# Softcap attention and two mixers on one core: the second block of keys added onto the first by a transfer, the softmax sums in three passes

## The chip, the core and the metric

The kernel runs on one core of one Trainium2 chip. The core has five engines, each with its own queue of instructions, which it works through in order: TensorE (PE, matrix products), VectorE (DVE), ScalarE (ACT), GpSimd (POOL) and SyncE (SP), which here issues transfers. Sixteen DMA engines move data between HBM and SBUF, the on-chip memory. The metric is the device time of one execution in microseconds; less is better.

## The reference

Three layers follow each other. This is the first, the one that the change touches, for 4 batches, 12 heads, 448 positions and 64 channels per head:

```python
scores = scale * np.matmul(q, k.transpose(0, 1, 3, 2))
scores = cap * np.tanh(scores / cap)
scores = scores - np.max(scores, axis=-1, keepdims=True)
attn = np.exp(scores)
attn = attn / (np.sum(attn, axis=-1, keepdims=True) + 1e-09)
return np.matmul(attn, v).astype(np.float32)
```

The second layer mixes tokens and then channels by two pairs of matrices each with a ReLU between; the third takes the real part of a two-dimensional Fourier transform, normalises, and applies two more matrices, 768 to 3072 and back. All is float32.

## The kernel before

Attention works on 12 quads, four heads each: a quad is one batch and a third of its heads, held as two pairs. The 448 keys stand on the partitions, in three blocks of 128 (`KC = 3`) and a rest of 64, and the 448 queries run along the free dimension. The first three blocks of a pair lie in one tile `t` of shape [128, 3, 2, 448] (block, head of the pair, query); the rests of both pairs share one tile `te`. There are four buffers for `t`, so two quads can be under way.

For each pair, TensorE makes the scores of one block of both heads (line 630, tile `sc`), ScalarE takes the tanh out of PSUM into `t` (line 616). VectorE takes the maximum over the blocks (through line 435, tile `m`), GpSimd takes it over the partitions, one all-reduce per head (line 670, tile `mb`), VectorE subtracts (line 435) and ScalarE takes the exponential in place (line 678). Then TensorE makes two products from the exponentials:

- the values (`av`, line 731, one product per pair, 12 matmuls of 32 columns of weights; line 741 adds the rest keys of both pairs);
- the softmax sums (`den`, line 766, one product per quad). Its weights `marks` hold ones in chosen columns, so that each of the four heads' sums over the keys lands in 32 partitions of its own. It runs over the three blocks and the rest: four passes of four matmuls.

ScalarE copies both out of PSUM (tile `xt`), TensorE turns the results (line 785), VectorE divides by the sums (line 823). As batches are finished, the token mixer of the second layer runs between the quads (lines 404 to 406 in `mix1` with tile `mx`, lines 886 and 890 in `mix2`). The channel mixers and the transform follow; they hold three quarters of the time, almost all of it matrix products of lines 404 to 406 with tile `mm`.

The order of all work is written down. Each piece is recorded with `pl.op`, with what it reads and writes; a table `ORDER` of 4192 numbers gives the sequence in which the pieces are issued, and a set `POOLED` names the pieces that GpSimd does where two engines could. The costs in `pl.op` (`{"T": 3.0}`, `lag=2.1`) do nothing when the program is built; the table was drawn up with them. Within an engine the instructions run in the order of the table, each waiting for what it reads and for its buffers to come free.

Of the kernel before, what the change touches and what calls it, by code (L numbers as in the profile page):

```python
# [16 lines left out]
ALU = mybir.AluOpType  # L17
# [7 lines left out]
KC = 3  # L25
# [33 lines left out]
class Op:  # L59
# [305 lines left out]
def kernel(  # L365
# [17 lines left out]
    V, A, P, T = nc.vector, nc.scalar, nc.gpsimd, nc.tensor  # L383
# [159 lines left out]
    def phase_ab(heads, mixer, banks_a, banks_b):  # L543
# [210 lines left out]
        def normed(stage, b, q, eks, te, sums):  # L754
            ps = ps_new(av_p, "av", [128, 512])
            twin = q < 2
            at = (32, 0, 16)[q]
            stage("den")

            def den(e):  # L760
# [1410 lines left out]
```

## Time and profile before

| | |
|---|---|
| time, median of 3 runs (lowest, highest) | 1335.45 us (1333.64, 1335.49) |
| profiled execution, its own time | 1332.71 us |
| its span, first to last instruction | 1330.6 us |
| mean granted TensorE clock | 0.999 of 2.4 GHz |
| PE busy | 1311.3 us, 99% |
| DVE busy | 992.6 us, 75% |
| ACT busy | 773.4 us, 58% |
| POOL busy | 479.5 us, 36% |
| DMA | 239.20 MB, mean 180 GB/s |

How to read it: the profile is of one execution, so its times are compared with its own 1332.71 us, 2.1 us over the span, and not with the median. Busy time of an engine leaves out register, semaphore and DMA-issuing instructions. Matmuls are pipelined and their ends are modelled, so the mean duration of one record is longer than the time by which it moves the next one back; where several follow each other, the pieces of the chain of waits, which lie end to end, give the time that they take together. A float32 matmul has two records, so `x24` of the value product are 12 matmuls. Matmuls on the rounded format (lines 404 to 406 and 890) and the turns have one.

### The profile page before, as it was taken

To read this page: it belongs to the slowest core of one execution; us is meant where nothing else is said; L and a number is where in the kernel's file an instruction comes from. 1 tells how busy PE (TensorE), PEld (TensorE's weight loads), DVE (VectorE), ACT (ScalarE), POOL (GpSimd) and SP (SyncE) were. 2 spreads that over 40 slices of the span, in tenths; PEclk is the share of its full clock that TensorE was granted. 3 is DMA by queue.
4 is the path that set the end of the run, shared out by engine and by line. 5 is a ranking of instruction groups with operands and counts; after the bars stand their busy time and mean duration, and the time that the engine had idled before them with its cause. 6 is when DMAs were issued, how large, how long until landed. Compare 5 with 4: busy or idle time off the path is not lost.

```text
span 1330.6 us, 18417 instructions
## 1 busy us (share of the span) xinstructions
PE 1311.3 (99%) x7214; PEld 1094.2 (82%) x7214; DVE 992.6 (75%) x1038; ACT 773.4 (58%) x934; POOL 479.5 (36%) x244
## 2 busy tenths in 40 slices
PE   7999999999999999999999999999999999999998
PEld 3345454589999999999999999999999999999997
DVE  7998888746655666577998866757889738558798
ACT  8898887778667666454545424553554454544432
POOL 4443426112322011323323554634533544412322
PEclk9999999999999999999999999999999999999999
DMA  4222211056888888997766753455565743323332
GB/s 164 104 88 96 68 57 42 1 196 223 314 293 299 268 304 276 325 308 261 293 215 233 252 183 109 141 177 184 185 217 174 268 146 100 122 100 109 105 108 83
DMA packets 74328, 239.20 MB, mean 180 GB/s; under 512 B 8354, under 2 KB 10274, under 8 KB 74114
## 3 DMA queue, kind: packets, MB, share of 16 engines
q1 hardware_dynamic: 74240, 238.03, 51.7%
q8 instruction: 57, 0.93, 0.3%
q14 instruction: 29, 0.24, 0.0%
q10 hardware_dynamic: 2, 0.00, 0.0%
HBM read 171.77 MB, written 69.56 MB: 181 GB/s over the span
## 4 chain that ended last, share of the span: by engine, by line
PE 84%; DVE 7%; ACT 5%; POOL 2%; DMA 2%; issue 1%; SPq 0%; POOLq 0%; DVEq 0%; ACTq 0%
PE mm L404 24%; PE mm L405 24%; PE mm L406 24%; PE sc L630 2%; PE av L731 2%; DVE t L435 2%; DVE m L435 2%; PE mx L890 2%; POOL mb L670 1%; ACT t L616 1%; ACT t L678 1%; PE av L766 1%; PE av L785 1%; DMA kept<-p 1%; PE mx L886 1%
## 5 line engine op out<-in xcount | busy, mean ns | idle before, releaser
L435 DVE TENSOR_TENSOR z<-mm,z 128x896 f32<-128x896 f32 (+1 forms) x207 | 198.8, 976 | 86.9 <-PE mm L406 83.2
L405 PE MATMUL mm<-u,wh 128*128 128x448 f32 x564 | 206.1, 365 | 0.0
L404 PE MATMUL mm<-u,wh 128*128 128x448 f32 x552 | 201.9, 366 | 0.0
L406 PE MATMUL mm<-u,wl 128*128 128x448 f32 x552 | 201.7, 365 | 0.0
L406 PE MATMUL mm<-r,wl 128*128 128x448 f32 x498 | 182.1, 366 | 1.1 <-DMA wl<-kept 1.1
L404 PE MATMUL mm<-r,wh 128*128 128x448 f32 x498 | 182.3, 366 | 0.7 <-DVE z L435 0.4
L435 POOL TENSOR_TENSOR p<-p 128x768 f32<-128x768 f32 (+1 forms) x47 | 91.9, 1955 | 246.6 <-DMA kept<-p 87.5
L405 PE MATMUL mm<-r,wh 128*128 128x448 f32 x462 | 169.0, 366 | 0.0
L670 POOL PARTITION_ALL_REDUCE mb<-m x48 | 105.2, 2239 | 148.4 <-DVE m L435 118.2
L432 ACT ACTIVATE r<-mm 128x896 fp32r<-128x896 f32 (+5 forms) x87 | 71.3, 829 | 144.4 <-PE mm L406 124.8
L405 PEld LDWEIGHTS mm<-u,wh 128*128 128x128 f32 x564 | 106.0, 188 | 8.7
L404 PEld LDWEIGHTS mm<-u,wh 128*128 128x128 f32 x552 | 103.6, 188 | 8.7
L406 PEld LDWEIGHTS mm<-u,wl 128*128 128x128 f32 x552 | 103.7, 188 | 8.5
L406 PEld LDWEIGHTS mm<-r,wl 128*128 128x128 f32 x498 | 93.5, 188 | 9.3 <-DMA wl<-kept 1.5
L404 PEld LDWEIGHTS mm<-r,wh 128*128 128x128 f32 x498 | 93.5, 188 | 9.0 <-DVE z L435 0.8
L432 ACT ACTIVATE cv<-raw 128x768 bf16<-128x768 int8 (+2 forms) x76 | 67.6, 889 | 52.0 <-DMA raw<-in_m_dram 39.6
L405 PEld LDWEIGHTS mm<-r,wh 128*128 128x128 f32 x462 | 86.8, 188 | 7.8 <-DVE r L966 0.7
L435 DVE TENSOR_TENSOR t<-t,mb 128x1344 f32<-128x1344 f32 x48 | 82.0, 1721 | 10.5 <-POOL mb L670 10.2
L405 PE MATMUL mm<-u,raw 128*128 128x448 f32 x246 | 89.8, 365 | 0.0
L435 POOL TENSOR_TENSOR wl<-wl,wh 128x768 fp32r<-128x768 f32 x29 | 58.7, 2030 | 72.6 <-ACT wh L432 72.6
L404 PE MATMUL mm<-u,raw 128*128 128x448 f32 x216 | 79.0, 366 | 0.3 <-DVE z L435 0.3
L406 PE MATMUL mm<-u,raw 128*128 128x448 f32 x216 | 78.9, 365 | 0.0
(245 smaller groups left out, 3011.8 us busy)
## 6 DMA issues: line engine op xcount, KB each, us to landing
raw<-in_m_dram SPq DMA_DIRECT2D x48, 768.0 KB, 6.3
kept<-p SPq DMA_DIRECT2D x96, 384.0 KB, 5.0
wl<-kept SPq DMA_DIRECT2D x82, 384.0 KB, 3.6
raw<-kept SPq DMA_DIRECT2D x53, 384.0 KB, 3.1
raw<-in_c_dram SPq DMA_DIRECT2D x24, 768.0 KB, 6.2
p<-kept SPq DMA_DIRECT2D x35, 384.0 KB, 4.0
qr<-in_qk_dram SPq DMA_DIRECT2D x23, 448.0 KB, 4.7
wh<-kept SPq DMA_DIRECT2D x24, 384.0 KB, 5.1
```

Of the source, the lines that this page charges most:

```text
L404: T.matmul(out=dst, lhsT=wh, rhs=xh, start=first, stop=False, skip_group_check=more)
L405: T.matmul(out=dst, lhsT=wh, rhs=xl, start=False, stop=False, skip_group_check=more)
L406: T.matmul(out=dst, lhsT=wl, rhs=xh, start=False, stop=last, skip_group_check=more)
L432: pl.op(a(n), lambda e: A.activation(out=out(), in_=src(), func=func, **kw), reads, writes)
L435: pl.op(engs, lambda e: eng[e].tensor_tensor(out=out(), in0=in0(), in1=in1(), op=op), reads, writes)
L616: pl.op(a(W2, 0.06), lambda e: A.activation(out=out(), in_=ps()[:, :, :S], func=AF.Tanh, scale=scl[:, 0:1]), [ps, "cap", *reads], writes)
L630: T.matmul(out=ps()[:, k, :S], lhsT=qr()[d, S + c * 128:S + (c + 1) * 128], rhs=qr()[d, :S], start=True, stop=True)
L670: pl.op({"P": 1.9}, lambda e, k=k: P.partition_all_reduce(mb()[:, k], mx()[:, k], 128, bass_isa.ReduceOp.max), [mx, mb], [kb], hold=0.75)
L678: pl.op(a(KC * S, 0.1), lambda e, k=k: A.activation(out=tl()[:, :, k], in_=tl()[:, :, k], func=AF.Exp, scale=cap_sb[:, 0:1]), [tl, "cap"], ...
L731: T.matmul(out=ps()[d, :S], lhsT=vv()[:, KC * p + c, d], rhs=tl()[:, c, hd], start=(c == 0), stop=False, skip_group_check=True)
L766: T.matmul(out=ps()[32 * k:32 * k + 32, :S], lhsT=w, rhs=tl()[:, c, hd] if c < KC else te()[:, hd], start=(c == 0), stop=(c == KC))
L890: T.matmul(out=ps()[:, :S], lhsT=channels_of(rt()[:, tb, c], kc % NJ), rhs=wt[:, tb, :], start=False, stop=last, skip_group_check=True)
```

## The change

After the value products of a quad, two transfers are issued from GpSimd's queue, one per pair. Each adds `t[:, 1]`, the exponentials of the second block of keys, onto `t[:, 0]`, those of the first, in SBUF (`accum_op=ALU.add`, 128 partitions of 896 numbers, 448 KB). The sums product then runs over block 0, block 2 and the rest: three passes, 12 matmuls. The value product needs the first block unsummed, so the transfer waits for it (through the key `(t, "sum")`, which the value product reads and the transfer writes) and for the two exponentials; the sums product waits for both transfers.

```diff
 POOLED = {
-    23, 26, 32, 35, 82, 85, 91, 94, 139, 142, 148, 151, 214, 217, 223, 226, 281, 284, 290, 293, 338, 341, 347, 350,
...
+    23, 26, 32, 35, 46, 47, 84, 87, 93, 96, 107, 108, 143, 146, 152, 155, 166, 167, 220, 223, 229, 232, 243, 244, 289,
...
-                pl.op({"T": 2.25}, av, [vv] + [x for tl, hd, ke in ts for x in (tl, ke)], [ps], mode="cols")
+                pl.op({"T": 2.25}, av, [vv] + [x for tl, hd, ke in ts for x in (tl, ke)] + [(ts[0][0], "sum")], [ps], mode="cols")
...
             at = (32, 0, 16)[q]
+            stage("pre")
+            sums_in = []
+            for ts in eks:
+                (tl, _, k0), (_, _, k1) = ts
+                pl.op({"P": 0.7}, lambda e, tl=tl: P.dma_start(out=tl()[:, 0], in_=tl()[:, 1], accum_op=ALU.add),
+                      [tl, k0, k1], [(tl, "sum")], lag=4.0)
+                sums_in.append((tl, "sum"))
             stage("den")
 
             def den(e):
-                for c in range(KC + 1):
+                for c in (0, 2, KC):
...
-            pl.op({"T": 3.0}, den, [te, (te, "e")] + [x for ts in eks for tl, hd, ke in ts for x in (tl, ke)], [ps], mode="cols")
+            pl.op({"T": 2.3}, den, [te, (te, "e")] + sums_in + [x for ts in eks for tl, hd, ke in ts for x in (tl, ke)], [ps], mode="cols")
```

`ORDER` has 4216 numbers now, 24 more for the transfers, and was drawn up anew, so the sequence differs over the whole kernel. Lines of the changed kernel have numbers higher by 2 up to the transfer (line 764 there) and by 9 after it. Three places matter most.

The first is TensorE around the sums product of the first quad: `av` the values, `te` the rest keys, `marks` the sums, `sc` scores of later quads. Before:

```order
L731 MATMUL av<-t,v 32x448 x12
L630 MATMUL sc<-qr 128x448 x4
L731 MATMUL av<-t,v 32x448 x12
L741 MATMUL av<-te,v 64x448 x4
L766 MATMUL av<-t,marks 32x448 x12
L766 MATMUL av<-te,marks 32x448 x4
L630 MATMUL sc<-qr 128x448 x2
```

The same place of the changed kernel:

```order
L733 MATMUL av<-t,v 32x448 x12
L632 MATMUL sc<-qr 128x448 x2
L733 MATMUL av<-t,v 32x448 x12
L743 MATMUL av<-te,v 64x448 x4
L632 MATMUL sc<-qr 128x448 x6
L775 MATMUL av<-t,marks 32x448 x8
L775 MATMUL av<-te,marks 32x448 x4
L632 MATMUL sc<-qr 128x448 x2
```

Three score steps (6 matmuls) have moved in between the second value product and the sums product.

The second place is TensorE in the fourth quad, where the token mixer's products (`mx`) run between. Before:

```order
L731 MATMUL av<-t,v 32x448 x12
L741 MATMUL av<-te,v 64x448 x4
L630 MATMUL sc<-qr 128x448 x2
L766 MATMUL av<-t,marks 32x448 x12
L766 MATMUL av<-te,marks 32x448 x4
```

The same place of the changed kernel:

```order
L733 MATMUL av<-t,v 32x448 x12
L632 MATMUL sc<-qr 128x448 x2
L895 MATMUL mx<-ident,x 128x112 x4
L899 MATMUL mx<-w2h,rh 128x448
L899 MATMUL mx<-w2h,rl 128x448
L899 MATMUL mx<-w2l,rh 128x448
L899 MATMUL mx<-w2h,rh 128x448
L899 MATMUL mx<-w2h,rl 128x448
L899 MATMUL mx<-w2l,rh 128x448
L743 MATMUL av<-te,v 64x448 x4
L632 MATMUL sc<-qr 128x448 x2
L775 MATMUL av<-t,marks 32x448 x8
```

A score step and a whole output block of the mixer stand there in addition. In the other quads the filling is of the same kind: score steps (two matmuls each), turns (four matmuls of line 794 there), mixer products. From the end of the second value product to the sums product stand, in quads 3 to 12: 12 mixer products of the first kind, `te` and 2 score steps; 1 score step, 1 output block, `te`, 1 step; 1 step, 1 block, `te`, 2 steps; `te`, 2 steps, 12 first-kind products, 4 turns; 1 step, 1 block, `te`, the rest's step; 12 first-kind products, 1 step, `te`, 1 step; 1 block, `te`, 2 steps, 4 turns; 1 step, 12 first-kind products, `te`, 1 step; 1 step, `te`, 1 block, 12 first-kind products; `te` and 2 blocks.

The third place is GpSimd's queue from the first to the fourth quad; `mb` is an all-reduce, its number that of the pair. Before:

```order
L670 ISA mb_339<-m2_323 128x448 x2
L670 ISA mb_378<-m2_348 128x448 x2
L670 ISA mb_454<-m2_401 128x448 x2
L670 ISA mb_486<-m2_443 128x448 x2
L670 ISA mb_570<-m2_507 128x448 x2
L670 ISA mb_620<-m2_568 128x448 x2
L670 ISA mb_769<-m2_697 128x448 x2
```

The changed kernel, from the second quad on:

```order
L672 ISA mb_477<-m2_407 128x448 x2
L672 ISA mb_488<-m2_453 128x448 x2
L764 DMA t_357<-t_357 128x896
L764 DMA t_411<-t_411 128x896
L672 ISA mb_567<-m2_493 128x448 x2
L672 ISA mb_615<-m2_569 128x448 x2
L764 DMA t_480<-t_480 128x896
L672 ISA mb_746<-m2_695 128x448
L764 DMA t_546<-t_546 128x896
L672 ISA mb_746<-m2_695 128x448
L672 ISA mb_828<-m2_754 128x448 x2
```

The transfers of a quad stand after its own all-reduces and before or between those of the next quad. Six times in the kernel one stands between the two halves of a pair, as here in `mb_746`.

## Rows read from the trace of the kernel before

**Rows 1.** The page, part 1: busy us, share of the span, instructions per engine.

```profile
PE 1311.3 (99%) x7214; PEld 1094.2 (82%) x7214; DVE 992.6 (75%) x1038; ACT 773.4 (58%) x934; POOL 479.5 (36%) x244
```

**Rows 2.** Windows of four stretches: length, busy (count) per engine, clock, DMA share.

```profile
0.00:52.00 52.00, 43.19 (x263) 15.19 (x263) 40.83 (x36) 42.69 (x48) 24.21 (x20) 0.97 0.41 141
52.00:275.00 223.00, 220.38 (x1650) 112.36 (x1649) 185.59 (x190) 178.64 (x211) 82.20 (x38) 1.00 0.18 62
275.00:1290.00 1015.00, 1012.54 (x5137) 935.12 (x5136) 730.54 (x772) 539.63 (x660) 363.07 (x182) 1.00 0.61 211
1290.00:1331.00 41.00, 35.20 (x171) 31.50 (x169) 35.61 (x43) 12.48 (x17) 10.06 (x5) 0.99 0.24 87
```

**Rows 3.** The chain that ended last, 52 to 150 us: start, length, what.

```profile
65.66 0.37 PE mx L404
...
70.02 2.39 PE av L731 x24
72.42 0.91 PE av L741 x8
73.33 0.95 PE sc L630 x4
74.28 3.14 PE av L766 x32
...
79.40 0.91 PE sc L651 x8
...
81.26 0.58 PE av L785 x4
81.84 1.71 PE sc L630 x8
...
99.43 0.54 PE mx L886 x4
99.96 1.23 PE mx L890 x6
```

**Rows 4.** Line L766: records, ns min/median/max, first and last start.

```profile
L766 PE MATMUL av<-t,marks x288: 535/539/564, 33.2 to 268.4; 128*32 128x448 f32 x144
...
L766 PE MATMUL av<-te,marks x96: 539/539/540, 35.5 to 269.1; 128*32 128x448 f32 x96
```

**Rows 5.** ScalarE's timeline at 77 us: start, length, instruction.

```profile
77.93 1.90 ACT L616 ACTIVATE t<-sc,scl 128x896 f32<-128x896 f32 x2
```

**Rows 6.** DMA queue and issues, 52 to 275 us: count, size, us to landing.

```profile
q1 hardware_dynamic: 3962, 13.50, 17.7%
...
qr<-in_qk_dram SPq DMA_DIRECT2D x15, 448.0 KB, 4.1
v<-in_vP_dram SPq DMA_DIRECT2D x9, 448.0 KB, 3.4
```

**Rows 7.** SyncE's timeline at 82 us: the issue of one load.

```profile
81.56 0.42 SPq L586 DMA_DIRECT2D v<-in_vP_dram  x1
```

**Rows 8.** DMA issues of the whole span: the slowest and the fastest landing.

```profile
kept<-wl SPq DMA_DIRECT2D x12, 384.0 KB, 7.4
...
kept<-y SPq DMA_DIRECT2D x2, 448.0 KB, 2.7
```

**Rows 9.** Line L670, the all-reduce: nanoseconds min/median/max.

```profile
L670 POOL PARTITION_ALL_REDUCE mb<-m x48: 1602/1844/5038, 12.9 to 254.1; - x48
```

**Rows 10.** GpSimd's timeline at 69 us: two all-reduces of one pair.

```profile
68.95 4.92 POOL L670 PARTITION_ALL_REDUCE mb<-m  x2 [9.90 <-DVE m L435]
```

**Rows 11.** What VectorE waited for, 0 to 275 us.

```profile
DVE t L435 <- POOL mb L670: 10.2, 8, 1.7
```

**Rows 12.** The chain that ended last near 180 us.

```profile
179.38 2.31 POOL mb L670
181.71 2.29 DVE t L435
```

446 rows, old and new, of tables (ORDER, POOLED) are left out of this document.

## The prediction

> **What bounds the kernel now.** I read the page's busy times first, then the windows by stage, then the chain of waits, then the DMA issues. TensorE is busy 1311.3 us of the 1330.6 us span, the other engines 75% or less [rows 1]. The windows say where the missing 19 us lie: 8.8 us in the first 52 us, 2.6 us from 52 to 275 us, 2.5 us in the thousand microseconds after that, 5.8 us in the last 41 us (length less busy PE) [rows 2]. All twelve quads of heads, and so the whole change, lie before 275 us. There TensorE is busy 220.4 of 223 us, VectorE 186, ScalarE 179, GpSimd 82, and the rows of the chain shown from there are all TensorE's [rows 2, 3]. So a microsecond less of TensorE work in that stretch is worth a microsecond, and a microsecond in which TensorE stands still costs one.
>
> **What is removed.** The product for the softmax sums takes 3.14 us for its 16 matmuls (x32, since the profile shows two records of each) [rows 3]; its records are alike, 539 ns each, whichever of its 288 and 96 records one takes [rows 4]. One of its four passes is therefore 3.14 / 4 = 0.785 us. Twelve quads lose one each: 9.4 us. Ten of these quads stand after 52 us, where the engine is full: 7.85 us. The first two stand in the stretch with 8.8 us of idle time, and I count half of their 1.6 us.
>
> **What is added: a transfer and a wait on it.** In each quad GpSimd issues two transfers, one per pair of heads, each adding 448 KB of the second block of keys onto the first. It may start only when the value product (av) of its pair has read the first block, and the sums product has to wait until it has landed. Behind that product on TensorE stand the next scores, turns and mixer products, all in order, and ScalarE's next tanh waits too, for its buffer: in the trace the first tanh of a later quad starts at 77.93 us, half a microsecond after the sums product ended at 77.42 us [rows 3, 5]. So the question is one comparison per quad: how long from the end of the second pair's av to the landed sum (call it L), against the TensorE work that the new order puts in between (call it D).
>
> D comes from the new order with durations of the chain [rows 3]: the last product with the rest keys 0.91, one score step (2 matmuls) 0.95, two 1.71, the score step of the rest 0.91, four turns 0.58, twelve mixer products of the first kind 4.36 / 2 = 2.18 (24 of them run from 65.66 to 70.02), one output block of the second kind 0.54 + 1.23 = 1.77. Quads 1 and 2 have 3.6 us each (three score steps and the 0.91). Quads 3 to 12 have, in order, 4.8, 4.6, 5.3, 5.4, 4.5, 5.0, 5.0, 5.0, 5.8 and 4.5 us, 5.0 in the mean. Before the change it was 1.86 us in quad 3 (72.42 to 74.28).
>
> L is not in the trace, since no accumulating transfer and none from GpSimd's queue is. I build it from four parts.
> - A load of the same 448 KB takes 3.4 us (v) to 4.1 us (qr) from issue to landing in this stretch, where the DMA engines are 17.7% busy [rows 6]. I take 3.4.
> - An accumulating transfer has to read both blocks. The 3962 packets of the stretch took 17.7% of 16 engines' 223 us, 0.159 us each; a transfer of 128 rows gives each engine eight, so a second read is 1.3 us.
> - GpSimd has to write out the transfer first. SyncE needs 0.42 us for a load [rows 7], which is inside the 3.4. The nearest GpSimd row is its shortest all-reduce, 1.6 us [rows 9]; I take that in place of the 0.42, so 1.2 us more.
> - GpSimd may be in an all-reduce when av ends: busy 82 of 223 us, each 2.2 us long, gives 0.37 x 1.1 = 0.4 us in the mean.
>
> Together L = 6.3 us. The bounds are far off: below, the fastest landing of this size in the whole trace and no queue, 2.7 us; above, the slowest, 7.4 us, with the second read, a 1.6 us issue and the longest all-reduce ahead of it (5.0 us), 15 us [rows 8, 9]. I stay near the loads of the same stretch, because they are the same size, the same rows and the same quiet engines.
>
> The stall is what L exceeds D by: at 6.3 us it is 1.5, 1.7, 1.0, 0.9, 1.8, 1.3, 1.3, 1.3, 0.5 and 1.8 us, 13.1 us for quads 3 to 12. In quads 1 and 2 it is 2.7 us each, 5.5 us, of which I count half, since there TensorE has idle time that it can replace; less half of the 1.6 us saved this is +2.0 us. These stalls have no cover otherwise: the engine is full on both sides.
>
> **The rest of the order.** The table was drawn up anew, so instructions are moved and buffers change hands in the later stages too. TensorE keeps the same number of products there, and it stood idle 2.5 + 5.8 us after 275 us [rows 2]. A new order can win at most that, and I have no row by which it should lose; 0, give or take 3 us.
>
> **Sum.** -7.85 + 13.1 + 2.0 = +7.3 us on the profiled execution of 1332.7 us (span 1330.6 and 2.1 around it). The median of the three runs shown is 1335.45 us, and from there it is 1343 us. Each microsecond on L is worth about 11 us above 5.8 us (ten stalls and half of two), less below, and next to nothing under 4.5 us. Equal times come at L = 5.6 us: 6.3 us of stalls in ten quads and 1.2 us from the first two, against 7.85 us.
>
> The Trainium skill ("DMA: Bandwidth & Descriptors", Anatomy of one DMA) puts a transfer from GpSimd's queue at 2.0 us plus its bytes at 436 GB/s, 3.05 us for 448 KB; "Collectives: The Full Stack" (The bandwidth ceiling) says that an add is slow only because it reads two sources on one ring, which makes it 4.1 us. The load's 3.4 us does not contradict the first, and no run so far shows the second. By these, estimated, L would be 4.5 us with the wait for GpSimd, and the sum -7 us: that is the first rival.
>
> **Rivals.**
> 1. *The transfer is hidden.* L stays under 4.6 us, because the write-out is short and the two reads overlap. Then the sums product never waits in quads 3 to 12, and the saving stays: -7.85 us, or -9.4 with the first two, so 1326 to 1328 us. For it: loads land in 3.4 us, the fastest transfer in 2.7 us, and the DMA engines are idle four fifths of the time. Against it: a second read is not free, and GpSimd is slower than SyncE at most things. It decides from L < 5.3 us on. Chance 0.31.
> 2. *A draw.* L between 5.3 and 5.9 us, by the same sum 1332 to 1338 us. Chance 0.17.
> 3. *The forecast.* L between 5.9 and 8 us; at 8 us the stalls in quads 3 to 12 are 30 us and the time is about 1361 us. Chance 0.37.
> 4. *GpSimd's queue becomes the wait.* In six places the order puts a transfer between the two all-reduces of the next pair, so the second all-reduce stands behind a transfer that waits for TensorE. In quad 4 of the trace the pair starts at 68.95 us and its second half at about 71.4 us [rows 10]; the av before it ends at 72.42 us, and with 1.6 us of write-out the second half would start at 74.0 us, 2.6 us late. VectorE's subtraction waits for all-reduces already (10.2 us in eight waits), and near 180 us that is the chain itself [rows 11, 12]. Six times 2.6 us is 16 us on top of the forecast: 1358 us. It decides where VectorE has nothing else to do at that moment; elsewhere its 83% load covers it. Chance 0.15.
>
> That the change does not do what it says I leave aside: the built program has twelve matmuls where there were sixteen, and 24 transfers on GpSimd.
>
> **How the numbers follow.** A measurement of this kernel tells 0.2% (2.7 us) from no change. Faster is rival 1, 0.31; same is the draw, 0.17; slower is the forecast and rival 4, 0.52. The likeliest single case is the forecast at L = 6.3 us, 1343 us; its own range is 1338 to 1361 us. The range has to reach to rival 1, since that holds much: 1326 at the lower end, and at the upper end 1366 us, which is rival 4 with a little more latency. Left out are L over 8.5 us and both delays together.
>
> **What would show it.** In the changed profile: the sums product has x24 records and 2.4 us instead of 3.14; the transfers stand under GpSimd's issues with a time to landing, 5 to 6 us if I am right, near 4 if rival 1 is; TensorE's list of waits gains one, the sums product waiting for the transfer, 10 to 25 us in total, and the busy PE of 52 to 275 us falls below 95%. In rival 4 VectorE's wait for the all-reduce grows well over 10 us. I am wrong in the main step if TensorE waits for these transfers less than 5 us in total, or if the time moves with no such wait and the difference lies after 275 us.

## The result, and the profile after

The changed kernel takes 1344.84 us (median of four runs, 1341.29 to 1345.47), the kernel before 1334.55 us in the same session (1332.53 to 1335.49). The ratio is 1.0080, with a 95% interval of 1.0066 to 1.0093: 10.3 us slower. The forecast was 1343 us. The time is close, but two terms of its sum were wrong, one too high and one left out, and nearly cancelled, as the experiments show.

The profiled execution took 1341.29 us with a span of 1339.5 us. The page's part 1 of the changed kernel (busy us, share, instructions per engine) answers to [rows 1]:

```profile
PE 1309.5 (98%) x7118; PEld 1090.2 (81%) x7118; DVE 998.3 (75%) x1040; ACT 773.9 (58%) x934; POOL 502.4 (38%) x266
```

TensorE has 96 records fewer and is busy 1.8 us less, and still the span is 8.9 us longer. The windows of the changed kernel, with the columns of [rows 2], say where:

```profile
0.00:52.00 52.00, 42.34 (x250) 14.64 (x252) 40.00 (x35) 42.53 (x48) 28.31 (x24) 0.93 0.59 168
52.00:275.00 223.00, 214.60 (x1534) 106.22 (x1534) 185.24 (x186) 175.57 (x206) 98.92 (x59) 1.00 0.41 106
275.00:1290.00 1015.00, 1009.51 (x5135) 930.81 (x5128) 729.63 (x765) 539.98 (x661) 364.65 (x179) 1.00 0.62 210
```

Between 52 and 275 us TensorE now stands idle 8.4 us instead of 2.6, and in the thousand microseconds after that 5.5 us instead of 2.5. In the first 52 us TensorE's mean granted clock is 0.93 of 2.4 GHz instead of 0.97: after ten microseconds in which it was busy for 7.3 in both kernels, it stood at the lower level, 1.2 GHz, for 6.8 us instead of 3.4, which can cost 1.7 us at most. The DMA engines' share in the attention went from 0.18 to 0.41 (next to last column). The transfers themselves, in the view of their line (nanoseconds min/median/max, first and last start; then who waited for them):

```profile
L764 POOL DMA_DIRECT2D t<-t x24: 862/900/1255, 25.1 to 268.1; - x24
...
  PEld av L775: 5.3, 3
  PE av L775: 2.9, 3
...
DMA to landing us min/median/max: 4.1/4.6/8.9
```

Only three waits of TensorE are put down to a transfer. Where they are, its timeline shows (start, length, engine, line, instruction, idle before):

```profile
118.98 0.95 PE L775 MATMUL av<-t,marks 128*32 128x448 f32 x4
121.02 1.32 PE L775 MATMUL av<-t,marks 128*32 128x448 f32 x10 [1.09 <-DMA t<-t]
...
165.78 0.95 PE L775 MATMUL av<-t,marks 128*32 128x448 f32 x4
168.32 1.32 PE L775 MATMUL av<-t,marks 128*32 128x448 f32 x10 [1.60 <-DMA t<-t]
...
189.49 1.71 PE L775 MATMUL av<-t,marks 128*32 128x448 f32 x16
```

The last row is quad 8, where the product runs through. From the first record's start to the last one's it needs 1.92 us then (2.67 us before the change). In quad 5 it needed 3.95, in quad 7 4.45, in quad 11 3.07 and in quad 12 2.02: 5.8 us of standing still inside this product, all told. In the other eight quads there is none.

### The profile page after: what moved, and what is told of

It is laid out like the page before. It is cut to its first block, busy times and chain, and to the rows that moved or that the text cites. A ratio compares the mean times of both kernels' runs of the same rounds, so it can differ in the third digit from the quotient of the medians.

```text
span 1339.5 us, 18331 instructions
## 1 busy us (share of the span) xinstructions
PE 1309.5 (98%) x7118; PEld 1090.2 (81%) x7118; DVE 998.3 (75%) x1040; ACT 773.9 (58%) x934; POOL 502.4 (38%) x266
## 4 chain that ended last, share of the span: by engine, by line
PE 80%; DVE 7%; ACT 5%; DMA 4%; issue 3%; POOL 1%; SPq 0%; ACTq 0%; DVEq 0%; POOLq 0%
PE mm L406 23%; PE mm L407 22%; PE mm L408 22%; DVE z L437 3%; PE av L733 3%; PE sc L632 2%; PE mx L899 2%; DMA t<-t 2%; PE av L775 2%; DMA raw<-in_m_dram 2%; ACT t L618 1%; ACT t L680 1%; PE av L794 1%; DVE t L437 1%; ACT cv L434 1%
## 5 line engine op out<-in xcount | busy, mean ns | idle before, releaser
L407 PE MATMUL mm<-u,wh 128*128 128x448 f32 x594 | 216.9, 365 | 0.0
L406 PE MATMUL mm<-u,wh 128*128 128x448 f32 x582 | 213.1, 366 | 0.9 <-ACT r L434 0.9
L408 PE MATMUL mm<-u,wl 128*128 128x448 f32 x582 | 212.6, 365 | 0.0
L406 PE MATMUL mm<-r,wh 128*128 128x448 f32 x474 | 173.5, 366 | 0.9 <-DVE z L437 0.7
L408 PE MATMUL mm<-r,wl 128*128 128x448 f32 x474 | 173.1, 365 | 0.0
L407 PE MATMUL mm<-r,wh 128*128 128x448 f32 x450 | 164.4, 365 | 0.0
L434 ACT ACTIVATE r<-mm 128x896 fp32r<-128x896 f32 (+4 forms) x86 | 70.4, 830 | 110.3 <-PE mm L408 86.2
L407 PEld LDWEIGHTS mm<-u,wh 128*128 128x128 f32 x594 | 111.6, 188 | 8.9
L406 PEld LDWEIGHTS mm<-u,wh 128*128 128x128 f32 x582 | 109.3, 188 | 10.3 <-ACT r L434 1.3
L406 PEld LDWEIGHTS mm<-r,wh 128*128 128x128 f32 x474 | 89.0, 188 | 9.7 <-DVE z L437 2.0
L407 PEld LDWEIGHTS mm<-r,wh 128*128 128x128 f32 x450 | 84.5, 188 | 7.0
L618 ACT ACTIVATE t<-sc,scl 128x896 f32<-128x896 f32 x72 | 70.8, 1003 | 15.1 <-PE sc L632 7.8
L434 ACT ACTIVATE wh<-wl 128x768 fp32r<-128x768 f32 x61 | 50.8, 840 | 49.4 <-DMA wl<-kept 49.2
L434 ACT ACTIVATE u<-u 128x896 fp32r<-128x896 f32 (+4 forms) x57 | 49.7, 900 | 51.3 <-DVE u L437 32.3
```

Source lines behind the costliest of these rows:

```text
L406: T.matmul(out=dst, lhsT=wh, rhs=xh, start=first, stop=False, skip_group_check=more)
L407: T.matmul(out=dst, lhsT=wh, rhs=xl, start=False, stop=False, skip_group_check=more)
L408: T.matmul(out=dst, lhsT=wl, rhs=xh, start=False, stop=last, skip_group_check=more)
L434: pl.op(a(n), lambda e: A.activation(out=out(), in_=src(), func=func, **kw), reads, writes)
L618: pl.op(a(W2, 0.06), lambda e: A.activation(out=out(), in_=ps()[:, :, :S], func=AF.Tanh, scale=scl[:, 0:1]), [ps, "cap", *reads], writes)
```

## The experiments

Two theories at the start, called W and O in what was expected. *Theory W*: the loss is TensorE waiting for landed sums, as forecast. *Theory O*: the loss is the new order itself, which the forecast put at 0 us. Times are set against the kernel before in the same session: 1334.09 us for the first four runs, 1332.63 for the next four, 1333.93 for three, 1333.54 for the last.

**The new order without the transfers.** order_four keeps the changed kernel's order (and its `POOLED`, by which VectorE has 1040 instructions instead of 1038), issues no transfer and makes all four passes. order_three keeps three passes and leaves the second block out of the sums.

```diff
-                pl.op({"P": 0.7}, lambda e, tl=tl: P.dma_start(out=tl()[:, 0], in_=tl()[:, 1], accum_op=ALU.add),
+                pl.op({"P": 0.7}, lambda e: None,
...
-                for c in (0, 2, KC):
+                for c in range(KC + 1):
```

order_three has only the first half of this edit. All other instructions stand as in the changed kernel.

> The changed order, but no transfers and the sums product with its four passes: the work of before in the sequence of after. Before took 1334.6 us, after 1344.8. Theory W (what costs is the wait for the transfers: three late landings hold TensorE 5.7 us, and the buffers and exponentials behind them come later): 1335 us, within 3. Theory O (the new order costs by itself: its value products wait for exponentials, about 8 us, and its later stages lose 4.3 us): 9.0 us of matmuls more than after and 5.7 us of stalls less, about 1347 us. In its profile the first product of the channel mixer starts at 278 us by W, at 286 us by O (before 278.5, after 283.1).

> The changed order with three passes and no transfers; the second block of keys is left out of the softmax sums, so this is the price of the change without its transfer. Theory W: the whole saving of 9.0 us on the time of before, 1326 us. Theory O: 1344.8 less the 5.7 us of stalls, 1339 us or a little less.

Measured: order_four 1344.71 us (1.0078, 1.0066 to 1.0090), 10.6 us over before, with not one transfer in it. order_three 1336.52 us (1.0016, 1.0006 to 1.0025). So the order alone costs 10.6 us, a pass less in twelve quads gives 8.2 back, and transfers with their waits, which stand between order_three (2.4 us over before) and the changed kernel (10.3 us over), cost 7.9. And 10.6 - 8.2 + 7.9 = 10.3 us is the whole difference; by the intervals each of these terms is known to about 2 us. Theory O had 1347 and 1339 us for the two runs, theory W 1335 and 1326. In order_four the first product of the channel mixer starts at 287.3 us, where O had 286 and W 278. Theory O is shown, beside W and not in its place.

A part of what the order costs can be read from the waits between 52 and 275 us (engine, line, tile it waited for: us in total, times, longest). The kernel before:

```profile
DVE m L435 <- ACT t L616: 4.8, 4, 3.1
...
ACT t L616 <- PE av L766: 0.3, 1, 0.3
```

And order_four:

```profile
DVE m L437 <- ACT t L618: 13.1, 11, 5.1
...
ACT t L618 <- PE av L775: 6.4, 3, 2.6
...
PE av L733 <- ACT t L680: 2.5, 3, 1.2
```

To be read from the middle row. The new order puts the sums product 5 us behind the value products instead of about 2. That product is the last reader of its quad's two `t` buffers, of which there are four, so ScalarE's tanh of a later quad now waits 6.4 us for it (0.3 before). VectorE's maximum waits for that tanh (13.1 us against 4.8), the exponentials come late, and the value product on TensorE waits 2.5 us for them, a wait that the kernel before does not have in this stretch. That is 2.5 of the 10.6 us. That the buffers held longer cause more of it is not shown: score steps, mixer blocks and loads stand elsewhere too, and the run that was to move the sums product alone (later_four, below) did not isolate it. Of the 14.0 us between the two profiled executions, 8.7 lie ahead of the channel mixer's first product and 5.3 behind it. In the first 52 us order_four has the changed kernel's lower clock (0.93). From 275 to 1290 us the changed kernel waits for VectorE:

```profile
PE mm L406 <- DVE z L437: 3.3, 4, 1.4
PE mm L407 <- DVE y L437: 1.1, 1, 1.1
```

The kernel before waits 0.4 us for `z` there and has no wait for `y`.

**The transfers without anybody waiting.** They add onto two spare tiles; the sums leave the second block out.

```diff
+        aside = [a1.tile([128, 2, S], F32, name="aside%d" % i) for i in range(2)]
...
-                pl.op({"P": 0.7}, lambda e, tl=tl: P.dma_start(out=tl()[:, 0], in_=tl()[:, 1], accum_op=ALU.add),
+                pl.op({"P": 0.7}, lambda e, tl=tl, i=i: P.dma_start(out=aside[i % 2], in_=tl()[:, 1], accum_op=ALU.add),
```

> The changed kernel, but each transfer adds onto a spare tile, so the traffic and GpSimd's 0.9 us each stay and the sums product waits for none of them; the second block is left out of the sums. Theory W: near the kernel without transfers, by which 1326 to 1331 us. Theory O: 1339 us. Rival T (not the wait but the traffic and GpSimd's lost time are the price): 1343 to 1345 us, as after.

Measured: 1336.55 us (1.0018, 1.0008 to 1.0028), as order_three, 2.5 us under O's figure and 6 us under the least that rival T had. Traffic and GpSimd's 0.9 us for each issue cost nothing that can be measured; the 8 us come from what waits for what. Two waits are gone here, that of the sums product for the landing and that of the transfer for the value product, so this run does not part them.

**The old order with the transfers.** old_order takes before's two tables, with each transfer right behind its value product.

In rows of TensorE in quad 4, a "-" for the changed kernel:

```diff
 L733 MATMUL av<-t,v 32x448 x12
-L632 MATMUL sc<-qr 128x448 x2
-L895 MATMUL mx<-ident,x 128x112 x4
...
 L743 MATMUL av<-te,v 64x448 x4
 L632 MATMUL sc<-qr 128x448 x2
 L775 MATMUL av<-t,marks 32x448 x8
```

> The order of before, with each transfer put straight behind its value product and three passes; the sums product stands where it stood, 1.6 to 2.8 us behind the second value product. An undisturbed transfer lands 3.3 us behind the end of the value product in the trace (4.1 from its issue), so each quad should stall about 1.2 us and three late landings some 2 us more: 12 x 1.2 + 6 - 9.0 = +11 us, 1346 us by W. By O, in which the old order is the better one in all else and the later buffers cost nothing, the same stalls but none of the 12 us of the order: also near 1346 us, and the later stages take the 1052 us of before, not 1056.

Measured: 1350.95 us (1.0125, 1.0110 to 1.0139), 5 us over the expectation. The sums product stands still 20.4 us by the same reckoning, and TensorE another 4.3 us right ahead of it in quads 9 and 10: 24.7 us. From the first product of the channel mixer on it takes 1052.5 us, the kernel before 1052.0, the changed kernel 1056.4: the later stages lose with the new order and not with the transfers. So the new order does cover most of the landing (5.8 us are left), and it is the better of the two with transfers, though not better than no change.

**The sums product alone moved later, in the old order**, with four passes and no transfers (later_four), and with three and transfers (later). What depends on it had to move with it. TensorE's rows in quad 3, a "-" for before, a "+" for later_four:

```diff
 L741 MATMUL av<-te,v 64x448 x4
-L630 MATMUL sc<-qr 128x448 x2
+L631 MATMUL sc<-qr 128x448 x4
+L793 MATMUL av<-ident,xt 112x128 x4
 L766 MATMUL av<-t,marks 32x448 x12
```

> The order of before in all but one thing: each sums product stands some 2 us of TensorE work later (2.9 to 6.1 us behind the second value product, where the changed order has 3.2 to 7.6); four passes, no transfers, so the same work as before. Theory L (the changed order's loss of 8.7 us in the attention comes from the later sums product, which holds the two pairs' buffers longer, so tanh and exponentials of the next quad but one come later): 6 to 9 us over before, 1340 to 1343 us. Rival M (it comes from everything else that the new table moved there): within 2 us of before, 1332 to 1336 us.

> The same with the transfers and three passes. Theory L: the loss of the run above, less 8.2 us of matmuls, and about 4 us of stalls in quads 1 to 3, which have only 2.9 to 4.1 us of work there, and on late landings: 1336 to 1339 us. Rival M: 1334 - 8 + 4 = 1330 us, faster than before.

Measured: 1392.94 us (1.0452, 1.0438 to 1.0465) and 1403.24 us (1.0528, 1.0513 to 1.0543). These are poor tests: in later_four TensorE's turns wait 22.9 us in eight places, up to 9.4 us at once, for the copies dragged along, and its mean granted clock is 0.87 in the first 52 us and 0.94 from 52 to 338 us, so it is at 1.2 GHz for long stretches. The 60.3 us can't be divided between the dragging, the clock and the place of the sums product, and theory L of these two expectations stays untested.

**Old order in the later stages, new order in the attention** (mixed). TensorE's rows are the changed kernel's up to the channel mixer; SyncE's change from the start, since its loads for later stages stand among those of the attention. Two of its places, a "-" for the changed kernel:

```diff
-L588 DMA qr<-in_qk_dram 128x896 x3
+L588 DMA qr<-in_qk_dram 128x896 x2
+L1024 DMA kept_124<-in_fft_dram 16x6272
+L588 DMA qr<-in_qk_dram 128x896
...
-L588 DMA qr<-in_qk_dram 128x896 x2
+L588 DMA qr<-in_qk_dram 128x896
+L467 DMA raw<-in_c_dram 128x6144
+L588 DMA qr<-in_qk_dram 128x896
```

> The changed kernel with the attention and token mixer in its own order and all later stages in the order of before. If the 4.4 us that the changed kernel loses behind 283 us are the order of the later stages, 1340 us, and those stages take 1052 us again; if they come from how the attention ends, 1345 us and 1056 us.

Measured: 1341.07 us (1.0061, 1.0042 to 1.0079). By the ratios that is 2.5 us better than the changed kernel, with intervals that overlap, and not for the reason tested: in the profiled executions the channel mixer and what follows take 1055.8 us against 1056.4, while the sums product stands still 1.7 us instead of 5.8, since quad 5 no longer waits. Near 300 us TensorE's granted clock falls to 1.2 GHz for 3.4 us (0.57 from 300 to 304 us, after five microseconds with 3.1 us of work), which can be 1.7 us of the 1055.8. Inconclusive on the later stages; loads placed otherwise spare a transfer.

**GpSimd does the addition itself**, in the old order with three passes.

```diff
-                pl.op({"P": 0.7}, lambda e, tl=tl: P.dma_start(out=tl()[:, 0], in_=tl()[:, 1], accum_op=ALU.add),
+                pl.op({"P": 0.7}, lambda e, tl=tl: P.tensor_tensor(out=tl()[:, 0], in0=tl()[:, 0], in1=tl()[:, 1], op=ALU.add),
```

> The order of before, three passes, and in place of each transfer a plain addition by GpSimd (128 x 896), straight behind the value product. GpSimd needs 2.15 us for such an addition elsewhere in the kernel, and the value product's end is told 0.8 us before its modelled end, so the sum is ready some 1.5 us behind it, and the sums product starts 1.9 to 2.8 us behind: theory W, that only the wait eats the saving: 1334 - 8 = 1326 us, up to 1329 with GpSimd busy at the wrong moment. Rival V (GpSimd's reads and VectorE's two-input subtractions and maxima hold each other up, 24 x 2.15 us on a VectorE that is busy 83%): 1335 us or more.

Measured: 1475.28 us (1.1063, 1.1046 to 1.1080), far above theory W and over rival V's floor, but not for rival V's reason: VectorE's subtraction takes 1.85 us in the mean instead of 1.72, which is 6 us for all 48, and its maxima together some 5.5 us longer. The waits of this kernel up to 430 us:

```profile
DVE t L436 <- POOL mb L671: 131.3, 15, 16.2
...
POOL mb L671 <- issue: 78.9, 13, 7.8
...
PE av L774 <- POOL t L763: 40.1, 10, 11.9
```

"issue" is time in which the engine waited for nothing that the profile shows. GpSimd stands so 78.9 us before 13 of its all-reduces, and its timeline shows when:

```profile
151.48 5.43 POOL L671 PARTITION_ALL_REDUCE mb<-m  x3 [5.92 <-issue]
164.00 4.85 POOL L763 TENSOR_TENSOR t<-t 128x896 f32<-128x896 f32 x2 [7.08 <-PE av L732]
176.64 3.23 POOL L671 PARTITION_ALL_REDUCE mb<-m  x2 [7.79 <-issue]
185.35 4.46 POOL L671 PARTITION_ALL_REDUCE mb<-m  x2 [5.48 <-DVE m L436]
```

Behind an addition the all-reduce comes 5.8 to 6.2 us late (7.8 in one place), behind another all-reduce it does not. VectorE's subtraction waits for the all-reduces 131.3 us. In each of the 13 gaps stand two `MODIFY_POOL_CONFIG` of GpSimd's. The all-reduce's line has 28 of them here; in the kernel before it has two, both at 2.1 us:

```profile
L671 POOLq MODIFY_POOL_CONFIG  x28: 1/6/12, 2.1 to 379.1; - x28
```

TensorE's clock adds to the loss. In the windows (columns of [rows 2]) it is 0.85 in this stretch, in which TensorE is busy 254.9 of 363 us:

```profile
57.00:420.00 363.00, 254.90 (x1617) 126.36 (x1614) 207.19 (x196) 187.51 (x220) 127.92 (x62) 0.85 0.12 40
```

So it runs at 1.2 GHz for some 109 us, which can be up to 54 us of the 141; how much of that lies in TensorE's way is not shown.

**Can the waits be taken out?** Two edits give the transfer more time without moving any instruction of TensorE. In last_pass the sums product reads the summed block last; in both_moves the transfer is moreover issued in the middle of its value product, behind the only third that reads the block it writes. Both stand in the old order, and both_moves_new_order has both in the new one.

```diff
+                        if c == 0:
+                            P.dma_start(out=ts[0][0]()[:, 0], in_=ts[0][0]()[:, 1], accum_op=ALU.add)
...
-                for c in (0, 2, KC):
+                for c in (2, KC, 0):
...
-                                 rhs=tl()[:, c, hd] if c < KC else te()[:, hd], start=(c == 0), stop=(c == KC))
+                                 rhs=tl()[:, c, hd] if c < KC else te()[:, hd], start=(c == 2), stop=(c == 0))
```

last_pass has the last two pairs of lines alone.

> The order of before with three passes and transfers right behind their value products (the run old_order), but the sums product takes its pass over the summed block last instead of first, so TensorE asks for the landed sum only after two passes. Those are two thirds of 2.36 us, 1.57 us later in each quad. Theory (what the changed order pays is bought to cover the landing; in before's order the loss is nothing but TensorE waiting for the sum): old_order stands 26.5 us of added waiting above before in the stretch up to the channel mixer, 2.2 us a quad, and 1.57 us of each goes, 12 x 1.57 = 19 us: 1332 us. Rival (a good part of old_order's loss is GpSimd's queue: all-reduces standing behind transfers that wait for TensorE, which a later pass does not touch): 1340 to 1347 us, and VectorE's wait for all-reduces above before's 10 us.

> As last_pass, and each transfer is issued already when the value product has read the first block (its first 4 of 12 matmuls), since only that block is written: two thirds of a value product of 2.1 us, 1.4 us earlier. Nothing else moves. Theory: from last_pass's 1332 us the remaining 0.6 us a quad goes too, and what is left is before less a pass in each quad: 1334.1 - 8.2 = 1326 us (1325 to 1330, a few tenths where a landing takes 7 to 9 us instead of 4.1); TensorE waits for the transfers less than 2 us in all. Rival (GpSimd's queue): no better than last_pass, 1335 us or above, because the transfers stand in the same place of the queue.

> The changed kernel in its own order, with the two moves of both_moves: summed block last in the sums product, transfers issued after the first third of their value product. Theory (the changed order costs 10.6 us of itself, the waits 8.3 us): the waits go, 3 us more slack in each quad against overhangs of at most 2.5 us, and the time is that of order_three, 1336.5 us (1335 to 1338): the cover that the changed order was to give is no longer needed and its price is still paid. Rival (the 8.3 us between order_three and the changed kernel are not waits for the landing but collisions of the transfers with loads or GpSimd's time): 1341 to 1345 us, as before the two moves.

Measured: 1353.41 us (1.0148, 1.0133 to 1.0163), 1352.54 us (1.0149, 1.0132 to 1.0167) and 1345.24 us (1.0089, 1.0072 to 1.0106). My theory fell in all three; the rivals' figures held for the last two, and last_pass came out above both. The standing still at the sums product did shrink: from 24.7 us in old_order to 11.1 and 10.8, and from 5.8 us in the changed kernel to 1.3. The times did not fall. both_moves also shows that its first edit starts no transfer earlier: 18 of the 24 start 0.8 to 1.0 us before their value product ends, and so do 16 in the changed kernel, where they are issued behind the whole product. So there, too, the transfer does not wait for the product's end: most start 0.3 us before the product's last record does.

In the old order a part of what was won went into other waits and into the clock. TensorE's waits ahead of its turns are 8.5 us in last_pass, 4.1 us in old_order. And after stretches with little work its granted clock falls to 1.2 GHz, as the windows of last_pass show:

```profile
80.00:82.00 2.00, 0.56 (x4) 0.32 (x4) 2.00 (x3) 1.98 (x3) 0.00 (x0) 0.97 0.00 0
82.00:89.00 7.00, 6.62 (x24) 2.88 (x26) 6.01 (x9) 4.52 (x6) 3.19 (x2) 0.52 0.38 120
...
235.00:245.00 10.00, 5.87 (x44) 1.46 (x36) 9.94 (x5) 5.18 (x7) 9.10 (x6) 1.00 0.68 139
245.00:253.00 8.00, 7.90 (x40) 4.76 (x44) 3.98 (x6) 4.31 (x7) 0.00 (x0) 0.79 0.00 0
```

Between 52 us and the channel mixer it is at 1.2 GHz for 13.7 us in last_pass and both_moves, 6.8 in old_order, and not at all in the kernel before, the changed kernel and order_four; against old_order that can be 3.4 us.

Where the 4.5 us won in the new order went, the timeline of both_moves_new_order shows at quad 11:

```profile
230.20 2.95 POOL L672 PARTITION_ALL_REDUCE mb<-m  x1 [2.70 <-DVE m L437]
...
238.95 2.46 PE L733 MATMUL av<-t,v 128*32 128x448 f32 x24
...
240.58 0.90 POOL L736 DMA_DIRECT2D t<-t  x1 [7.43 <-issue]
241.18 1.90 POOL L672 PARTITION_ALL_REDUCE mb<-m  x1
243.11 1.56 DVE L437 TENSOR_TENSOR t<-t,mb 128x1344 f32<-128x1344 f32 x1 [4.70 <-POOL mb L672]
243.11 0.95 ACT L434 ACTIVATE mb<-mb 64x896 f32<-64x896 f32 x1 [4.52 <-POOL mb L672]
...
245.15 2.40 PE L632 MATMUL sc<-qr 64*128 64x448 f32 x8 [3.73 <-ACT t L618]
```

Issuing from inside the value product moved the transfer ahead of an all-reduce in GpSimd's queue. GpSimd ends one all-reduce at 233.15 us and stands 7.43 us before the transfer, which waits for a value product that starts at 238.95 us. The second all-reduce of the pair stands behind it, VectorE waits 4.70 us for that and ScalarE's copy of the maxima 4.52 us. ScalarE's next tanh stands behind this copy, and TensorE's next scores wait 3.73 us for the tanh. After this gap the granted clock falls to 1.2 GHz for 6.8 us (columns of [rows 2]):

```profile
240.00:245.00 5.00, 1.41 (x16) 0.26 (x8) 1.56 (x1) 1.86 (x3) 2.50 (x2) 1.00 0.47 92
245.00:250.00 5.00, 3.75 (x16) 1.00 (x20) 3.64 (x4) 5.00 (x6) 0.00 (x0) 0.65 0.00 0
250.00:255.00 5.00, 5.00 (x32) 1.10 (x24) 3.00 (x2) 2.34 (x4) 3.95 (x3) 0.67 0.47 92
```

That is up to 3.4 us more; with the 3.73 us it outweighs the 4.5 us won. The changed kernel's clock does not fall there, and its own order has both all-reduces ahead of the transfer there:

```profile
231.97 4.55 POOL L672 PARTITION_ALL_REDUCE mb<-m  x2 [1.91 <-DVE m L437]
...
244.76 2.84 POOL L672 PARTITION_ALL_REDUCE mb<-m  x1 [8.24 <-DVE m L437]
...
247.47 1.81 POOL L764 DMA_DIRECT2D t<-t  x2
```

It pays with a first transfer that starts 4.3 us after its value product was done, and with 1.15 us of standing still in quad 11's sums product, less than the two losses above.

**GpSimd's queue in the old order put right** (behind_reduces): last_pass with the transfers of six quads behind an all-reduce that is ready sooner, and in quad 10 the other way. GpSimd's rows of quad 4, a "-" for last_pass:

```diff
 L763 DMA t<-t 128x896
-L671 ISA mb<-m_883 128x448
-L763 DMA t<-t 128x896
-L671 ISA mb<-m_883 128x448
+L671 ISA mb<-m_883 128x448 x2
+L763 DMA t<-t 128x896
```

> The run last_pass (before's order on TensorE, VectorE and ScalarE, summed block last in the sums product) with nothing changed but GpSimd's queue: in seven places a transfer that stood ahead of an all-reduce which is ready sooner by the trace of before goes behind it (quads 2, 3, 4, 6, 7, 9), and in quad 10 the first transfer goes ahead of an all-reduce. Theory Q (GpSimd's queue is what the changed order pays to avoid: in last_pass VectorE's subtraction waits 14.2 us for all-reduces against before's 8.7, the all-reduces of quads 4, 6 and 10 start 5 to 7 us late behind transfers that wait for TensorE, and TensorE's stalls of 2 to 6 us near 80, 146 and 238 us follow): most of the 27 us of added stalls go, and the time is before less a pass plus what the slow landings of quads 6 and 10 leave, 1326 to 1334 us, with VectorE's wait for all-reduces back under 10 us. Rival W (the landing itself, 4.1 to 9 us, is what before's order cannot cover): 1344 to 1353 us, with TensorE's wait for the transfers still above 7 us.

Measured: 1350.22 us (1.0132, 1.0112 to 1.0152), where the rival had it, though the mechanism of theory Q is visible. From 52 to 300 us VectorE's wait for all-reduces falls from 14.2 us to 10.3 (8.7 before). TensorE's standing still in the sums products rises from 11.1 us to 17.4, since the transfers now come late. Its timeline at quad 9:

```profile
213.73 2.85 POOL L671 PARTITION_ALL_REDUCE mb<-m  x1
...
216.45 0.91 POOL L763 DMA_DIRECT2D t<-t  x1
...
217.33 0.95 PE L774 MATMUL av<-t,marks 128*32 128x448 f32 x4
...
223.56 1.71 PE L774 MATMUL av<-t,marks 128*32 128x448 f32 x4 [5.28 <-DMA t<-t]
```

The transfer went out at 216.45 us behind an all-reduce that ran late itself, landed 7.1 us later, and the last pass waited 5.28 us for it. So in the old order GpSimd's queue can favour the all-reduces or the transfers, and one of them is then late; all four arrangements end between 1350 and 1354 us. No run here beats the kernel before.

## Why the prediction was right in the time and wrong in its terms

**The pass removed: right.** It was put at 0.785 us a quad; the trace shows 2.67 us before and 1.92 us after from the product's first record to its last, 0.75 us. Forecast in all 8.65 us (7.85 and half of the first two quads' 1.6), measured 8.2 us between order_four and order_three.

**D, the cover: right.** Forecast for quads 3 to 12 were 4.5 to 5.8 us. From the end of the second value product to the start of the sums product the trace after shows 4.8, 4.9, 5.4, 5.3, 4.7, 5.0, 5.0, 5.1, 5.8 and 4.5 us, none more than 0.3 us from its forecast.

**L, the latency: sized wrong.** Forecast were 6.3 us from the end of the value product. Undisturbed, a transfer lands 4.1 us after its issue starts, and the issue starts some 0.8 us before the value product ends: 3.3 us. Two parts were wrong. The transfer does not wait for the whole value product, as I let it, though I had written that it waits for the reading of the first block. And I added 1.3 us for the second read and 1.2 for the writing out, while 4.1 us contains GpSimd's 0.9 us and leaves 3.2, where a load's 3.4 less its 0.42 leaves 3.0 [rows 6, 7]. The second read is there in the engines' time, 2.4 us of each engine for a transfer against a load's 1.3, but an undisturbed landing is hardly longer for it. The Trainium skill ("DMA: Bandwidth & Descriptors", Anatomy of one DMA, with "Collectives: The Full Stack", The bandwidth ceiling, for the second read) gave an estimate of 4.1 us for such a transfer; with the undisturbed landings the trace agrees. It agrees in the total; that the second read takes a microsecond of it no run shows.

With 3.3 us rival 1 would hold in every quad. It does in nine, to 0.1 us; in quads 5, 7 and 11 a landing took 7.3 to 8.9 us, in quad 11 with no load beside them, where the two transfers went out 0.6 us apart. Why quad 5 is slow can be seen in the DMA issues between 105 and 122 us (tile, engine, count, KB each, median us to landing; ahead of them the queues' packets, MB and share of 16 engines):

```profile
q1 hardware_dynamic: 1005, 3.54, 61.1%
q0 software_dynamic: 288, 0.92, 27.4%
...
qr<-in_qk_dram SPq DMA_DIRECT2D x4, 448.0 KB, 6.7
...
t<-t POOLq DMA_DIRECT2D x2, 448.0 KB, 8.5
```

and between 178 and 190 us, in quad 8:

```profile
q0 software_dynamic: 288, 0.92, 39.2%
q1 hardware_dynamic: 72, 0.20, 5.1%
...
t<-t POOLq DMA_DIRECT2D x2, 448.0 KB, 4.1
```

Next to SyncE's loads the same two transfers take 8.5 us instead of 4.1, and the loads 6.7 us where they took 4.1 before [rows 6]. The forecast had taken the stretch's mean share of 17.7% for every quad. So the stalls are few and long, where the sum had many short ones: 5.8 us directly and 7.9 us with what follows from them, against 15.9 us (13.1 and half of 5.5). The list of waits gives 2.9 us to the matmuls and 5.3 to the weight loads before them, the product's own records 5.8: far from the 10 to 25 us forecast, and by the first figure under the 5 us at which the forecast called itself wrong in the main step. The busy share of 52 to 275 us is 96.2%, where I expected less than 95.

**"The rest of the order", 0 give or take 3 us: wrong.** This is the step that failed. Measured are 10.6 us, where the forecast had "no row by which it should lose". It did have the mechanism of a part in hand, that ScalarE's tanh waits for the buffers that the sums product reads, and counted it in the stall alone. But a sums product that is put off by 3 us on purpose holds its buffers just as long as one that waits 3 us, so D is no free cover: in order_four the tanh waits 6.4 us for that product without any transfer. How much of the 10.6 us this is stays open. [Rows 5] did not show such a wait, as the forecast read it: that tanh follows ScalarE's own copy without a gap, and the kernel before has 0.3 us of it in the whole stretch:

```profile
77.49 0.54 ACT L432 ACTIVATE xt<-av 128x448 f32<-128x448 f32 x1
```

**Rival 4, GpSimd's queue: not in the changed kernel.** VectorE's wait for the all-reduces between 52 and 275 us fell to 4.0 us, from 8.7 before. order_four, without transfers, has the same 4.0 us: the fall comes with the order, and the transfers add nothing to it. As a mechanism it is real, as both_moves_new_order shows: 4.7 us of VectorE's time at one place.

**The sum.** Forecast -8.65 + 15.85 + 0 = +7.3 with the roundings, measured -8.2 + 7.9 + 10.6 = +10.3. That the time came out right was luck: an overestimate of 8 us met an omission of 10.6 us. The direction was luck too, since the two terms that the forecast weighed against each other come to -0.3 us, and the loss is the term put at 0.

Open is what holds the old order at 1350 to 1354 us in detail, since no run took the late transfers, the late all-reduces and the lower clock away together; what the two moves would give the changed kernel with GpSimd's queue left alone (only the summed block last), which was not run; and how the 10.6 us of the order divide beyond the waits shown, in the later stages above all.

## What to carry to other kernels

Work that is put between a transfer and its reader is cover only for the reader; whatever the reader holds (here two of four buffers) is held longer by the same time, and the new order can cost elsewhere too, so time it without the transfer before crediting it. Size a transfer's latency by the busiest quad and not by the stretch's mean share of the DMA engines, and count each queue it is put into: an engine that issues a transfer behind a wait keeps everything after it. And removing a wait that the profile names can give nothing when the edit moves an instruction in another in-order queue, or when TensorE's clock falls after a gap that is left: read the granted clock of the stretch before pricing a wait.

## What the runs showed of the hardware

- An accumulating transfer of 448 KB within SBUF lands 4.1 us after its issue starts on GpSimd, 0.9 us of it the issue, when nothing else moves; 5 to 10 us beside loads or beside a second one (up to 8.9 us in the changed kernel, 10.3 in old_order). All 24 took 4.3% of 16 engines' 1339.5 us, 2.4 us of all engines each; by estimate two at once hold the engines for 4.8 us.
- 24 such transfers whose result nobody waits for cost nothing (aside against order_three, 1336.55 and 1336.52 us).
- GpSimd stands idle 5.8 to 7.8 us before an all-reduce that follows a tensor addition (78.9 us in 13 places), with two `MODIFY_POOL_CONFIG` in each gap and nothing in the profile that it waits for; an all-reduce behind an accumulating transfer shows no such gap, as at 241.18 us above.
- TensorE's granted clock fell from 2.4 to 1.2 GHz for 6.8 us after it had stood 3.73 us in both_moves_new_order (0.65 and 0.67 from 245 to 255 us); the value product at 248.65 us needs 3.96 us for 20 records there, where the one at 238.95 us needs 2.46 us for 24.
